# A new order for the opening of a fused gated-recurrence and ELU kernel

## The chip, the cores and the metric

The kernel runs on one NeuronCore of one Trainium2 chip. The metric is the device time of one execution in microseconds. Three timed runs of the kernel before took 670.13, 671.49 and 674.26 us; their median is 671.49.

A core has five engines that run their own instruction lists in order and meet at semaphores: TensorE (PE; its weight loads are shown as PEld), VectorE (DVE), ScalarE (ACT), GpSimd (POOL) and SyncE (SP), which issues most of the DMAs.

## The reference

The inputs q, k, v, a_re and a_im have the shape 4 x 8 x 768 x 48 (batch, head, time, feature), and the weights are 384 x 2048 and 2048 x 384. The weights arrive as 64-bit floats.

```python
mag = np.sqrt(a_re * a_re + a_im * a_im)
scale = np.minimum(mag, 0.999) / (mag + 1e-06)
a_re_n, a_im_n = a_re * scale, a_im * scale
for t in range(S):
    ar, ai = a_re_n[:, :, t, :, None], a_im_n[:, :, t, :, None]
    S_re, S_im = ar * S_re - ai * S_im + outer(k[t], v[t]), ar * S_im + ai * S_re
    y[:, :, t] = q[:, :, t] @ S_re
x = y.transpose(0, 2, 1, 3).reshape(3072, 384)
h = x @ w_in
out = np.where(h > 0, h, np.exp(np.minimum(h, 0)) - 1) @ w_out
```

The first part is a linear recurrence with a complex decay per step and feature. The second is a two-layer network with an ELU between the layers.

## The kernel before

**Units.** The work is cut into 12 units. A unit is 128 time steps of two batches, thus 256 rows of x. For a unit u the kernel turns the recurrence into products within chunks of 64 steps and a state that is carried from chunk to chunk. Its steps are small functions, each called with u and, where a unit is done by halves, the batch n:

- load_a, load_qk, load_v: DMAs from SP (L598).
- squares, joined, logarithms, powers, lengths, ratios, slopes (L705 to L780): the logarithm of the decay's size and the tangent of its angle, on ScalarE and VectorE. noted (L791) checks the range of the inputs on ScalarE.
- angles (L811 or L815): the arctan, on ScalarE. carried (L826) adds the turns that the unit before left.
- decays (L932 or L889, with the exponentials L920 or L904): sums over time as products with a triangular matrix, then the exponentials of both signs.
- turns (L837 on TensorE, L842 to L849 on VectorE): the sums of the angles; carry_on (L862) keeps the last row for a later unit with a DMA from POOL.
- waves (L973 to L977): sine and cosine on ScalarE. ends (L946 to L954): the decay over a whole chunk, as small products, two small copies and a product.
- scaled (L982 to L992) and gated (L1003): q and k times decay and wave, on VectorE.
- transposed (L1023, copies L1024), scores (L1031, mask L1036), states (L1064, sums L1077 to L1081), values (L1100 and L1109, copies L1121 and L1126): the attention-like products. scored and valued are the forms of unit 2 and later, which treat both halves together (L1136, L1145, L1177).
- seam (L1190): DMAs that put the last features of a head pair into the rows of x.

**The network.** For the first two units (u = 0, 1) the first layer is inner(u, f) on TensorE (L1210, 12 instructions of 128 x 256, two blocks of 128 hidden columns) and elu(u, f) (L1219, L1220 on ScalarE, L1221 on VectorE). project(u, n, f0, f1) adds the second layer for some blocks (L1235) and writes the output (copies L1243, DMAs L1244). Later units use sums of blocks that save products (mult L1455, product L1319, with sums of the weights in combined L1278 and summed_in L1403).

**Weights.** fetch loads a part of the 64-bit weights, and convert is one instruction of five on VectorE (L40, L43, L46, L50, L655) that round a part to 32 bits. There are 16 parts: eight of w_in, eight of w_out. inner(u, 2m) needs part m of w_in; a chunk of project needs two parts of w_out.

**Buffers.** PSUM holds three banks called w (transposes, scores, states, sums), three called mlp (inner, the projections of unit 0, sums and warm) and two called y (values, the projections of unit 1). inner(u, f) can only start when an elu has freed a bank.

**Order.** Nothing is scheduled by a planner in the opening. The list first (L1584) names the steps in the order in which they are written, and each engine's instruction list has its instructions in that order; an instruction that has to wait holds all that stand behind it on its engine. table (L1200) loads a set of ScalarE's functions ahead of use; where none is named, a load is put in before the function that needs it. warm (L1557) is some products of no use that keep TensorE's clock up. What the list doesn't name is appended from a second list with planned times (plan), in the order of those times; this is the steady part, from unit 3 on, of about 50 us per unit.

## Time and profile before

| | |
|---|---|
| median of three runs | 671.49 us |
| the profiled execution | 669.23 us |
| its span | 667.1 us |
| TensorE busy, share | 639.6 us, 96% |
| VectorE busy, share | 503.6 us, 75% |
| ScalarE busy, share | 419.2 us, 63% |
| GpSimd busy, share | 154.4 us, 23% |
| mean granted TensorE clock | 0.993 |
| first inner of unit 0 | 41.70 us |
| first inner of unit 1 | near 79 us |
| last convert on VectorE ends | near 128 us |
| first inner of unit 2 | near 164 us |

The profile is one execution, recorded in hardware. The span is from its first to its last instruction, and the profiled execution's own time is that and 2.1 us around it. A row of a timeline has its start and its duration in microseconds, engine, line, operation, what is written and read, the shape, how many instructions are merged, and in brackets the idle time of the engine before it with what ended it. Durations of one engine can overlap a little at their ends, so distances between starts are used for sums. The busy time of TensorE is modelled at the ends; a full TensorE need not be one at its peak.

### The profile page before, as it was taken

To read this page: it belongs to the slowest core of one execution; us is meant where nothing else is said; L and a number is where in the kernel's file an instruction comes from. 1 tells how busy PE (TensorE), PEld (TensorE's weight loads), DVE (VectorE), ACT (ScalarE), POOL (GpSimd) and SP (SyncE) were. 2 spreads that over 40 slices of the span, in tenths; PEclk is the share of its full clock that TensorE was granted. 3 is DMA by queue.
4 is the path that set the end of the run, shared out by engine and by line. 5 is a ranking of instruction groups with operands and counts; after the bars stand their busy time and mean duration, and the time that the engine had idled before them with its cause. 6 is when DMAs were issued, how large, how long until landed. Compare 5 with 4: busy or idle time off the path is not lost.

```text
span 667.1 us, 17231 instructions
## 1 busy us (share of the span) xinstructions
PE 639.6 (96%) x7236; PEld 579.6 (87%) x7236; DVE 503.6 (75%) x801; ACT 419.2 (63%) x684; POOL 154.4 (23%) x200
## 2 busy tenths in 40 slices
PE   8899899999999899999999999999999999999995
PEld 6777786576898798998998998999999999999995
DVE  5889999968777788678678768768768768765481
ACT  6885455874846567667677677677677577471250
POOL 2000000112124303503503503503603602402000
PEclk9799999999999999999999999999999999999999
DMA  9986645630900632452451451451551551212100
GB/s 166 189 142 105 148 149 167 112 72 20 154 3 15 115 56 62 81 106 57 86 106 53 90 104 48 97 104 44 100 104 44 102 104 43 54 32 61 34 2 29
DMA packets 151443, 56.12 MB, mean 84 GB/s; under 512 B 129684, under 2 KB 143164, under 8 KB 151356
## 3 DMA queue, kind: packets, MB, share of 16 engines
q1 hardware_dynamic: 147616, 53.58, 38.8%
q0 software_dynamic: 3520, 1.20, 1.5%
q8 instruction: 59, 0.97, 0.6%
q14 instruction: 28, 0.23, 0.1%
q10 hardware_dynamic: 220, 0.14, 0.1%
HBM read 48.91 MB, written 4.80 MB: 81 GB/s over the span
## 4 chain that ended last, share of the span: by engine, by line
PE 44%; DVE 10%; ACT 8%; issue 3%; DMA 1%; SPq 0%; ACTq 0%; DVEq 0%
PE mlp L1319 18%; PE mlp L1455 10%; PE y L1455 5%; DVE g L1471 3%; PE w L1023 3%; DVE g L1480 3%; PE y L1109 2%; ACT ee L1477 2%; ACT ee L1476 2%; PE w L1064 2%; PE w L837 2%; DVE g L1297 1%; ACT L735 1%; DVE n L772 1%; ACT n L746 1%
## 5 line engine op out<-in xcount | busy, mean ns | idle before, releaser
L1319 PE MATMUL mlp<-w_out,g 128*128 128x192 f32 x640 | 111.8, 328 | 1.0 <-DVE ee L1331 1.0
L1319 PEld LDWEIGHTS mlp<-w_out,g 128*128 128x128 f32 x640 | 104.2, 190 | 4.4 <-DVE ee L1331 1.6
L1081 POOL TENSOR_TENSOR S<-S,T 128x384 f32<-128x384 f32 x36 | 30.9, 857 | 175.5 <-DVE S L1079 175.5
L1210 PE MATMUL mlp<-x,w_in 128*128 128x256 f32 x288 | 65.1, 381 | 3.0 <-DVE g L1221 2.6
L1210 PEld LDWEIGHTS mlp<-x,w_in 128*128 128x128 f32 x288 | 53.8, 190 | 11.7 <-DVE g L1221 3.1
L1471 DVE TENSOR_TENSOR g<-g,mlp 128x512 f32<-128x512 f32 x45 | 30.7, 682 | 40.1 <-ACT qt L1024 28.7
L1297 DVE TENSOR_TENSOR g<-g 128x512 f32<-128x512 f32 x80 | 54.4, 695 | 5.0 <-PE mlp L1319 3.8
L1455 PE MATMUL mlp<-x,w_in 128*128 128x128 f32 x424 | 56.2, 275 | 0.4 <-DVE o L1344 0.4
L1480 DVE SCALAR_TENSOR_TENSOR g<-ee,g 128x512 f32<-128x512 f32 x63 | 47.6, 755 | 11.1 <-ACT ee L1477 11.0
L1319 PE MATMUL mlp<-w,g 128*128 128x192 f32 x320 | 54.5, 329 | 0.0
L1319 PEld LDWEIGHTS mlp<-w,g 128*128 128x128 f32 x320 | 51.8, 190 | 0.6
L1455 PEld LDWEIGHTS mlp<-x,w_in 128*128 128x128 f32 x424 | 51.6, 192 | 0.8 <-DVE o L1344 0.6
L1476 ACT ACTIVATE ee<-g 128x512 f32<-128x512 f32 x63 | 39.5, 627 | 17.2 <-DVE g L1471 16.7
L1190 POOL DMA_DIRECT2D x<-y x62 | 29.8, 488 | 87.2 <-ACT y L1126 37.3
L1468 ACT COPY g<-mlp 128x512 f32<-128x512 f32 x36 | 21.1, 586 | 44.0 <-PE mlp L1455 43.7
L1477 ACT ACTIVATE ee<-ee 128x512 f32<-128x512 f32 x72 | 45.4, 631 | 2.3
L1024 ACT COPY qt<-w 128x512 f32<-128x512 f32 x48 | 25.8, 589 | 15.5 <-PE w L1023 15.4
L973 ACT ACTIVATE cs<-n 128x768 f32<-128x768 f32 (+1 forms) x14 | 10.5, 751 | 38.0 <-DVE n L845 37.9
L904 ACT ACTIVATE n<-w 64x384 f32<-64x384 f32 (+1 forms) x60 | 28.1, 486 | 8.9 <-PE w L889 8.3
L1455 PE MATMUL mlp<-x,g 128*128 128x128 f32 x224 | 29.7, 275 | 1.2 <-DVE o L1344 1.2
L1219 ACT ACTIVATE ee<-mlp 128x512 f32<-128x512 f32 x24 | 14.3, 595 | 25.6 <-PE mlp L1210 17.2
L1455 PE MATMUL y<-x,w_in 128*128 128x128 f32 x216 | 29.0, 277 | 1.4 <-ACT g L1468 1.4
(222 smaller groups left out, 1434.8 us busy)
## 6 DMA issues: line engine op xcount, KB each, us to landing
w<-in_moe_w_out_dram SPq DMA_DIRECT2D x8, 768.0 KB
g<-in_moe_w_in_dram SPq DMA_DIRECT2D x24, 256.0 KB
g<-in_moe_w_out_dram SPq DMA_DIRECT2D x24, 256.0 KB
w<-in_moe_w_in_dram SPq DMA_DIRECT2D x16, 288.0 KB
vn<-in_v_dram SPq DMA_DIRECT2D x24, 192.0 KB
ar<-in_a_re_dram SPq DMA_DIRECT2D x22, 192.0 KB
ai<-in_a_im_dram SPq DMA_DIRECT2D x22, 192.0 KB
q<-in_q_dram SPq DMA_DIRECT2D x22, 192.0 KB
```

Of the source, the lines that this page charges most:

```text
L904: nc.scalar.activation(out=flat(x[key][to, n : n + 1]), in_=t[of], func=AF.Exp, scale=sign)
L1024: nc.scalar.copy(out=o[:, h0 : h0 + 4], in_=t)
L1081: eng.tensor_tensor(out=new_s, in0=new_s, in1=wide, op=ALU.mult)
L1190: eng.dma_start(out=x["x"][ds(j * HP + D, G), i], in_=x["y"][ds(j * HP + i * G, G)])
L1210: nc.tensor.matmul(t[:, e], lhsT=w_in[:, i, ts(f + e, C)], rhs=x["x"][:, i], start=(i == 0), stop=(i == NI - 1),)
L1297: nc.vector.tensor_tensor(out=S_of(u, k, h), in0=a, in1=b, op=op)
L1319: nc.tensor.matmul(to, lhsT=a[:, m], rhs=b[:, m], start=(first and h == 0 and m == 0), stop=False, skip_group_check=True,)
L1455: nc.tensor.matmul(x["c" + c][:, ts(m, C)], lhsT=a[:, m], rhs=x["mix"][p], start=(p == BANKS[c][0] and m == 0), stop=False, skip_group_che ...
L1471: nc.vector.tensor_tensor(out=part(u, to), in0=part(u, a), in1=part(u, b), op=op)
L1476: nc.scalar.activation(out=e, in_=part(u, of), func=AF.Relu, scale=-1.0)
L1477: nc.scalar.activation(out=e, in_=e, func=AF.Exp, scale=-1.0)
L1480: nc.vector.scalar_tensor_tensor(out=part(u, to), in0=nat[u]["e", to], scalar=-1.0, in1=part(u, of), op0=ALU.add, op1=ALU.max,)
```

## The change

Only the list first changes. The functions are the same, and the same steps are issued, each once, in another order:

- Unit 0: the halves of k are scaled in the other order and ahead of ends; a convert step stands ahead of gated; q of batch 0 is transposed first, then k of batch 0, q of batch 1; the natural_log set is loaded after the first two; states(0, 0) comes ahead of scores(0, 1); the logarithms of unit 1 come behind values(0, 0).
- Unit 1: slopes and angles come ahead of noted, and ends, turns and scaled ahead of inner(0, 0) and inner(0, 2). elu(0, 0) comes behind waves. The set trig_and_small is named ahead of waves for the units 1, 2 and 3. transposed(1, "q", 1) comes ahead of inner(0, 6).
- The first layer: elu(0, 4) comes ahead of seam(1); other elus and inners change places.
- The projections: unit 1's first two chunks come ahead of inner(1, 14) and unit 0's first; unit 1's last chunk of batch 1 comes ahead of unit 2's states.
- Unit 2: its four transposes stand next to each other. Unit 3: its turns and waves come later among the projections, its q and k loads behind the first outputs.
- The list goes on a little further, with steps of the units 2 to 4 that the plan put in nearly the same order before.

The core of the diff, with "..." where lines are left out:

```diff
-        (waves, 0, 1), (begun, 1), (warm, 1), (scaled, 0, "q", 0), (ends, 0), (scaled, 0, "k", 0),
-        (scaled, 0, "k", 1), (scaled, 0, "q", 1), (warm, 1), (gated, 0, 0), (warm, 1), (noted, 0),
-        (table, "natural_log"), (warm, 2), (gated, 0, 1), (warm, 2), *3 * [(convert,)],
-        (transposed, 0, "k", 0), (transposed, 0, "q", 1), (carry_on, 0), (transposed, 0, "q", 0),
-        *4 * [(convert,)], (scores, 0, 0), (transposed, 0, "k", 1), (scores, 0, 1), (load_a, 1),
-        (squares, 1), (joined, 1), (fetch, "in", 3), (logarithms, 1), (states, 0, 0),
-        (values, 0, 0), (powers, 1), (convert,), (states, 0, 1), (lengths, 1), (load_qk, 1),
-        (convert,), (ratios, 1), (values, 0, 1), (seam, 0), (warm, 2), (warm, 2), (decays, 1),
-        (load_a, 2), (warm, 1), (inner, 0, 0), *2 * [(convert,)], (noted, 1), (scaled, 1),
-        (warm, 4), (convert,), (load_v, 1), (slopes, 1), (ends, 1), *3 * [(convert,)],
-        (inner, 0, 2), (elu, 0, 0), (convert,), (fetch, "in", 4), (angles, 1), (turns, 1),
-        (waves, 1), (gated, 1, 0), (inner, 0, 4), (gated, 1, 1), (transposed, 1, "q", 0),
-        (transposed, 1, "k", 0), (convert,), (scores, 1, 0), (load_v, 2), (convert,),
...
+        (turned, 0, 1), (waves, 0, 0), (waves, 0, 1), (begun, 1), (scaled, 0, "q", 0), (warm, 1),
+        (scaled, 0, "k", 1), (scaled, 0, "k", 0), (ends, 0), (scaled, 0, "q", 1), (warm, 1),
+        (noted, 0), (convert,), (gated, 0, 0), (warm, 1), (warm, 2), (gated, 0, 1), (warm, 2),
+        (convert,), (transposed, 0, "q", 0), (convert,), (transposed, 0, "k", 0),
+        (table, "natural_log"), (carry_on, 0), (transposed, 0, "q", 1), (scores, 0, 0),
+        *3 * [(convert,)], (load_a, 1), (transposed, 0, "k", 1), (states, 0, 0), (scores, 0, 1),
+        (squares, 1), (joined, 1), (fetch, "in", 3), (convert,), (values, 0, 0), (logarithms, 1),
+        (powers, 1), (convert,), (states, 0, 1), (warm, 2), (load_qk, 1), (convert,), (lengths, 1),
+        (values, 0, 1), (ratios, 1), (seam, 0), (warm, 2), (decays, 1), (load_a, 2), (warm, 1),
+        (slopes, 1), (convert,), (angles, 1), (convert,), (noted, 1), (convert,), (ends, 1),
+        (load_v, 1), (convert,), (turns, 1), (scaled, 1), (inner, 0, 0), (convert,), (inner, 0, 2),
+        (fetch, "in", 4), (table, "trig_and_small", 1), (warm, 4), (waves, 1), (gated, 1, 0),
+        (convert,), (elu, 0, 0), (convert,), (transposed, 1, "q", 0), (gated, 1, 1),
+        (transposed, 1, "k", 0), (load_v, 2), (convert,), (inner, 0, 4), (convert,),
+        (fetch, "in", 5), (scores, 1, 0), (states, 1, 0), *2 * [(convert,)],
+        (transposed, 1, "k", 1), (convert,), (transposed, 1, "q", 1), (fetch, "in", 6),
+        (inner, 0, 6), *2 * [(convert,)], (elu, 0, 2), (convert,), (fetch, "in", 7), (scores, 1, 1),
+        (convert,), (values, 1, 0), (states, 1, 1), (values, 1, 1), *3 * [(convert,)], (warm, 2),
+        (elu, 0, 4), (seam, 1), (convert,), (inner, 0, 8), *2 * [(convert,)], (inner, 0, 10),
+        (elu, 0, 8), (convert,), (fetch, "out", 0), (elu, 0, 6), (convert,), (inner, 1, 0),
...
+        *3 * [(convert,)], (elu, 1, 12), *4 * [(convert,)], (project, 1, 0, 0, 4),
+        (project, 1, 1, 0, 4), (inner, 1, 14), (project, 0, 0, 0, 4), (logarithms, 2), (convert,),
...
+        (table, "trig_and_small", 2), *3 * [(convert,)], (project, 1, 0, 8, 12), *2 * [(convert,)],
+        (turns, 2), (project, 0, 1, 4, 8), (begun, 3), *2 * [(convert,)], (waves, 2), (squares, 3),
+        (scaled, 2), (ends, 2), (gated, 2), (joined, 3), (project, 1, 1, 8, 12),
+        (project, 1, 1, 12, 16), (logarithms, 3), (powers, 3), (states, 2, 0), (load_qk, 3),
+        (project, 1, 0, 12, 16), (lengths, 3), (ratios, 3), (project, 0, 0, 8, 12),
+        (transposed, 2, "k", 0), (transposed, 2, "q", 1), (slopes, 3), (transposed, 2, "q", 0),
+        (transposed, 2, "k", 1), (table, "trig_and_small", 3), (angles, 3), (scored, 2), (opened,),
+        (carried, 3), (project, 0, 1, 8, 12), (valued, 2), (seam, 2), (noted, 3),
+        (project, 0, 0, 12, 16), (summed_in, 0), (summed_in, 1), (combined, 1, 1), (turns, 3),
...
```

## The prediction

> **What bounds the kernel now.** I read the page's slices first, then TensorE's, VectorE's and ScalarE's instructions in order of time over the opening (0 to 165 us), the only part in which the change moves anything.
>
> The page, part 2, busy tenths of 40 slices of 16.7 us:
>
> ```profile
> PE   8899899999999899999999999999999999999995
> DVE  5889999968777788678678768768768768765481
> PEclk9799999999999999999999999999999999999999
> ```
>
> TensorE is full from the sixth slice to the end, so time is saved only where it idles, warms up or runs at half clock, which is in the first 104 us; from there on its order decides nothing unless a new hole opens. The stretches of 10 us (busy PE, PEld, DVE, ACT, POOL) show the second bound:
>
> ```profile
> 20.00:30.00 10.00, 8.67 (x73) 7.86 (x72) 9.79 (x14) 7.92 (x14) 0.00 (x0) 0.67 1.13 184
> 60.00:70.00 10.00, 9.34 (x265) 8.19 (x267) 9.58 (x15) 5.17 (x12) 0.00 (x0) 1.00 0.70 119
> 90.00:100.00 10.00, 10.00 (x48) 8.80 (x47) 9.79 (x15) 5.91 (x10) 0.00 (x0) 1.00 0.51 160
> ```
>
> From 50 to 130 us VectorE is 88 to 98% busy converting the weights (16 parts of 0.57 + 0.96 + 0.55 + 0.96 + 0.96 = 4.0 us) beside the units' gates. A change of order takes no work from it. The holes of TensorE, from its timeline:
>
> ```profile
> 41.70 3.06 PE L1210 MATMUL mlp<-x,w_in 128*128 128x256 f32 x12 [0.36 <-DMA x<-y]
> ...
> 55.44 1.09 PE L1023 MATMUL w<-ident,qg 128*128 128x128 f32 x8 [0.92 <-DVE qg L1003]
> ...
> 75.94 2.86 PE L1210 MATMUL mlp<-x,w_in 128*128 128x256 f32 x12 [2.65 <-DVE g L1221]
> 78.63 0.61 PE L1557 MATMUL mlp<-ident 128*128 128x128 f32 x4
> 79.08 23.48 PE L1210 MATMUL mlp<-x,w_in 128*128 128x256 f32 x108
> 103.98 2.85 PE L1235 MATMUL mlp<-w_out,g 128*128 128x384 f32 x8 [1.42 <-DVE g L1221]
> ```
>
> The two large holes end with VectorE's L1221 (the elu that frees an mlp bank). All gaps from 20 to 104 us add up to 8.8 us. On ScalarE:
>
> ```profile
> 46.07 1.28 ACT L815 ACT_TABLE_LOAD   x1
> 47.37 0.84 ACT L815 ACTIVATE n<-n 128x768 f32<-128x768 f32 x1
> 48.23 1.28 ACT L973 ACT_TABLE_LOAD   x1
> 52.70 0.52 ACT L973 ACTIVATE cs<-n 128x384 f32<-128x384 f32 x1 [3.19 <-DVE n L845]
> ```
>
> Unit 1's arctan (L815) stands behind noted and the first elu; its sine waits 3.19 us for the turns.
>
> **What the Trainium skill says.** "ScalarE: Activation LUTs", What ACT_TABLE_LOAD costs: a switch of set loads for about 1283 ns; the rows above show 1.28 us. "TensorE: Matmul & The Clock Gate", Part 1: the clock is halved after a window of some 3.4 us with TensorE idle and freed after a busy one; the trace agrees, with a granted clock of 0.50 from 20 to 26 us, right after the small products of ends at 16.55 to 19.3. "DMA: Bandwidth & Descriptors", Latency and other measured facts: about 2 us of fixed cost; the page's median for the seam's POOL copies (x<-y) is 2.0.
>
> **The change, part by part.** I lay the new order out with the old durations: VectorE by start-to-start distances (0.47 us for 384 columns, 0.87 to 0.99 for 768, 0.60 for an elu), TensorE 2.65 us for an inner or a project of four, 0.87 for a transposed; all from the rows of before.
>
> *Unit 0 (20 to 39 us).* q0 and k0 are transposed first, and the natural_log load goes behind their copies. The transposes run at half clock until 26.5 (1.73 us each instead of 0.87), so scores(0,0) starts at 27.1 for 27.70: 0.6 gained. Then states(0,0) goes ahead of scores(0,1), and unit 0's last product ends at 37.8 for 38.7. One convert step (0.55) ahead of gated is paid later anyway. But on ScalarE the copies of values(0,0), which wait for TensorE until 32.9, now stand ahead of unit 1's logarithms: L747 ends at 39.0 for 38.1, and the copies and seam of values(0,1) behind it come 0.8 late (issued 40.1 for 39.36). That is the new wait; behind it stand decays' exponentials, 41.6 for 40.9, after the two issues (1.50 us).
>
> *Unit 1 (39 to 60 us).* decays is even (39.7 for 39.66). slopes and angles come ahead of noted and elu(0,0): arctan ends at 45.3 for 48.2, the turns start on TensorE at 45.5 for 50.5, the waves end at 50.9 for 55.2, and gated(1,0) starts at 51.6 for 54.4. The named trig load replaces one that stood there, so no load is added (36 in the first 400 instructions of ScalarE in both). inner(0,0) and (0,2) now follow the turns, hence TensorE reaches the transposes at 52.8. inner(0,4) still goes ahead of scores(1,0): 57.4 for 57.75. Of almost 3 us only 0.35 is left at this place, and VectorE, which has done the same work, is level within 1 us. noted(1) ends at 47.4 for 44.5 and releases unit 1's a buffer, so the fetch of the fifth weight part goes out at 47.5 for 46.99: free, as its first use is at 62.
>
> *First layer (60 to 109 us).* values(1,1) ends at 70.1 for 70.5. The warm calls are as many as before, one pair only stands earlier. elu(0,4) now runs ahead of seam(1), so the bank that ended the 2.65 us hole is freed earlier: inner(0,10) at 73.7 for 75.94. The seam's three issues (2.73 us on ScalarE) follow it to 75.2, elu(0,8) is late by that, and inner(1,0) starts at 77.3 for 79.08. From here the free banks pace TensorE: VectorE ends the eighth part at 84.4 for 84.0, and inner(0,12), (0,14), (1,10) each wait 0.1 to 0.3 for an elu; inner(1,12) ends at 101.0 for 103.0. The 1.42 us hole goes, because two chunks of unit 1's projection (their weights converted by 93.3) stand where unit 0's chunk waited. After equal work (inner(1,14) and two chunks) TensorE is at 108.9 for 111.9: **3.0 us ahead.**
>
> *Unit 2 (109 to 164 us).* VectorE is as late as before: last convert 128.6 for 128.3, gated(2) for k ends 135.1 for 134.95. TensorE gets there at 135.0 with 11 chunks done for 10, so one chunk (2.65) is kept and the rest of the lead goes into the gate. Then the four transposes of unit 2 stand together, not among chunks. Three banks, emptied by copies of 0.54 us, stretch them and the state products behind them from 4.6 to 5.9 us, 1.3 lost for 0.5 before. Balance: 2.65 - 0.2 - 0.8 = **1.6 us**, inner(2,0) at 162.5 for 164.12. The seam of unit 2 is issued near 157 and lands before 161. Later gates keep up: waves(3) ends at 166.1 for 168.7.
>
> *Queues.* SP's order is the same up to unit 3's a loads. Then q and k of unit 3 go behind the outputs of the first half of unit 1: those copies end at 135.5, and the loads wait for gated(2) until 136.8 anyway (136.65 before). v of unit 3 and a of unit 4 go ahead of the last two outputs: earlier, and nothing waits for those outputs but the next o copies. POOL's carry of unit 3 goes behind the seam of unit 2 to about 161.5; its reader is at 202.6. If the cover of the q and k loads failed, their landing would still have 25 us before scaled(3).
>
> **Sum.** The profiled execution took 669.23 us (span 667.1, 2.1 around it); minus 1.6 gives 667.6. The median of the three runs is 2.3 above the profiled one and I shift by that: 671.49 - 1.6 = **669.9**. From 164 us the order is the old one and the lead passes through, as TensorE waits there under 4 us in all, for things that itself set going. Not shown by the trace is how many of the waits of 0.1 to 0.3 add up; with the lengths of copies and issues that makes 1.3 either way.
>
> **Rivals.**
> (1) *Larger gain, 667.0.* If the copies on ScalarE cost less than laid out and gated(2) ends before TensorE arrives, the lead of 3.0 at 109 us survives, and the small holes at 41.7 and 55.4 (1.3 together) go too: 4.3 to 4.5. For it: both large holes are attacked. Against: VectorE has no idle time to give, and it sets the gate at 135.
> (2) *Slower: a second half-clock stretch, 673.3.* Moving inner(0,0) behind the turns leaves TensorE from 41 to 45.5 us with one warm instruction and the small products of ends (L946), and an idle wait for the copy once; that is the pattern that came before the half clock at 20 us. A stretch like that one (6.7 us) loses up to 3.4 us of products (turns, inner(0,0), inner(0,2)): +3.4 - 1.6 = +1.8. It decides if over 3.2 us run at half clock with none of it hidden. Against: VectorE is the second bound, so half of it may be hidden, and then the result is rival 3.
> (3) *Nothing moves, 671.4.* The gate at 135 us comes 1.5 us later, as VectorE waits for late scores(1,0), and eats the chunk.
>
> **How the numbers follow.** Forecast 0.48, larger gain 0.17, slower 0.2, nothing 0.15. The forecast's own range is 668.6 to 671.2; rival 1's 667.0 and rival 2's 673.3 with the runs' own spread give 666.9 to 673.4. A measurement tells about 1% from no change (the runs before spread 0.6%), 6.7 us: no case reaches it, the largest conceivable gain (all 8.8 us of gaps) just would; I leave 0.03 for faster and 0.04 for slower from a hole that I don't see.
>
> **What would show it.** Right: turns of unit 1 near 45.5, gated(1,0) near 51.6, no hole above 1.5 us from 70 to 104, inner(1,0) near 77.3, states(2,0) near 135 with 11 chunks done, inner(2,0) near 162.5. Wrong: a granted clock of 0.5 after 43 us, ScalarE's copies holding scores, a wait for qg or kg at 135 of over 1 us, or a hole in front of the transposes of unit 3.

## The result, and the profile after

The changed kernel took 667.18 us (median; 665.14 to 668.96) where the kernel before took 670.23 us beside it (668.52 to 674.26), 20 runs each; the two medians are 3.05 us apart. The ratio of the two kernels is 0.9947, with a 95% interval of 0.9936 to 0.9959: a gain of 0.5%, or 3.5 us (2.8 to 4.3) of the median on record, where the prediction had 1.6. The direction and "within 1%" held. But 667.18 lies under the forecast's own range (668.6 to 671.2) and only within the wide one (666.9 to 673.4): the size was short by a factor of two. The profiled execution of the changed kernel took 665.7 us (span 663.7, before 669.23 and 667.1).

The same views as before the change. The page, part 2, in 40 slices of 16.6 us:

```profile
PE   8889999999999899999999999999999999999995
...
DVE  5798999967868689578678678678668768764481
...
PEclk9799999999999999999999999999999999999999
```

The stretches of 10 us (busy PE, PEld, DVE, ACT and POOL, then the granted clock):

```profile
20.00:30.00 10.00, 9.38 (x80) 8.85 (x79) 7.92 (x12) 7.62 (x14) 0.00 (x0) 0.70 1.19 176
60.00:70.00 10.00, 9.92 (x263) 8.52 (x260) 8.54 (x13) 4.25 (x10) 0.00 (x0) 1.00 0.53 100
90.00:100.00 10.00, 10.00 (x48) 8.80 (x47) 9.76 (x14) 6.17 (x10) 0.00 (x0) 1.00 0.48 156
```

In the first stretch TensorE is busier (9.38 for 8.67 us) but hardly further along (scores(0, 0) start at 27.20 for 27.70), for its clock is at half again (0.70 for 0.67). VectorE is less busy in the second (8.54 for 9.58), because it now waits for TensorE there:

```profile
60.81 0.69 DVE L1036 TENSOR_TENSOR a<-w,mask 128x512 f32<-128x512 f32 x1 [1.15 <-PE w L1031]
```

TensorE of the changed kernel in order of time (start, duration, then the idle time before the row and what ended it):

```profile
45.66 0.41 PE L953 MATMUL w<-once,pair 48*128 48x32 f32 x2 [1.94 <-DVE once L951]
46.00 2.43 PE L837 MATMUL w<-n,sum_turns 128*128 128x384 f32 x4
48.22 6.21 PE L1210 MATMUL mlp<-x,w_in 128*128 128x256 f32 x24
...
55.16 1.04 PE L1023 MATMUL w<-ident,qg 128*128 128x128 f32 x8
...
72.21 29.18 PE L1210 MATMUL mlp<-x,w_in 128*128 128x256 f32 x132
101.23 5.32 PE L1235 MATMUL y<-w_out,g 128*128 128x384 f32 x16
106.39 2.75 PE L1210 MATMUL mlp<-x,w_in 128*128 128x256 f32 x12
...
134.59 1.15 PE L1064 MATMUL w<-vn,kg 64*64 64x48 f32 x64
...
140.93 1.04 PE L1023 MATMUL w<-ident,kg 128*128 128x128 f32 x8
...
144.75 1.53 PE L1064 MATMUL w<-vn,kg 64*64 64x48 f32 x64
...
161.43 7.93 PE L1210 MATMUL mlp<-x,w_in 128*128 128x256 f32 x36
```

Four things are to be seen. The turns of unit 1 (L837) start at 46.00 instead of 50.48, but take 2.43 us for 1.45, and inner(0, 0) and inner(0, 2) behind them 6.2 us for 5.3: half clock. The transposes of unit 1 start at 55.16, before 55.44: of the 4.5 us by which the turns are earlier, 0.3 are left. From 72.21 us eleven inner steps stand in one row (132 products) without a hole; before, there was a hole of 2.65 us in this stretch and one of 1.42 us right behind it. And states(2, 0) starts at 134.59 with eleven chunks of the projections done, before at 135.01 with ten.

ScalarE, the arctan of unit 1 and its first sine:

```profile
44.49 0.84 ACT L815 ACTIVATE n<-n 128x768 f32<-128x768 f32 x1
...
48.62 0.52 ACT L973 ACTIVATE cs<-n 128x384 f32<-128x384 f32 x1
```

The arctan ends at 45.3 for 48.2 and the sine starts at 48.62 for 52.70, as laid out.

### The profile page after: what moved, and what is told of

Same layout as the page of the kernel before. It is cut to its first block, busy times and chain, and to the rows that moved or that the text cites. A ratio compares the mean times of both kernels' runs of the same rounds, so it can differ in the third digit from the quotient of the medians.

```text
span 663.7 us, 17229 instructions
## 1 busy us (share of the span) xinstructions
PE 640.6 (97%) x7236; PEld 580.2 (87%) x7236; DVE 501.9 (76%) x801; ACT 418.9 (63%) x684; POOL 153.8 (23%) x200
## 4 chain that ended last, share of the span: by engine, by line
PE 63%; DVE 14%; ACT 10%; issue 5%; DMA 4%; SPq 3%; DVEq 0%; ACTq 0%
PE mlp L1319 20%; PE mlp L1455 10%; PE mlp L1210 7%; PE y L1455 5%; PE w L1023 4%; DVE g L1471 4%; PE mlp L1235 3%; PE y L1235 3%; PE y L1109 3%; DVE g L1480 3%; SPq L598 3%; DMA w<-in_moe_w_in_dram 3%; PE w L1064 2%; PE w L837 2%; ACT ee L1477 2%
## 5 line engine op out<-in xcount | busy, mean ns | idle before, releaser
L1471 DVE TENSOR_TENSOR g<-g,mlp 128x512 f32<-128x512 f32 x45 | 30.6, 681 | 40.1 <-ACT qt L1024 28.6
L1455 PEld LDWEIGHTS mlp<-x,w_in 128*128 128x128 f32 x424 | 51.6, 192 | 0.7 <-DVE o L1344 0.6
L1190 POOL DMA_DIRECT2D x<-y x62 | 29.9, 489 | 94.8 <-ACT y L1126 43.5
L1468 ACT COPY g<-mlp 128x512 f32<-128x512 f32 x36 | 21.1, 585 | 43.9 <-PE mlp L1455 43.7
L1079 DVE TENSOR_TENSOR S<-w,S 128x384 f32<-128x384 f32 x38 | 21.0, 553 | 12.2 <-POOL S L1081 10.0
```

The source lines that it names most:

```text
L1190: eng.dma_start(out=x["x"][ds(j * HP + D, G), i], in_=x["y"][ds(j * HP + i * G, G)])
L1455: nc.tensor.matmul(x["c" + c][:, ts(m, C)], lhsT=a[:, m], rhs=x["mix"][p], start=(p == BANKS[c][0] and m == 0), stop=False, skip_group_che ...
L1471: nc.vector.tensor_tensor(out=part(u, to), in0=part(u, a), in1=part(u, b), op=op)
```

## The experiments

Two terms first. A chunk is one call of project, four blocks for one batch, 2.6 us of TensorE. The gate of unit 2 is the moment when VectorE has kg ready, without which states(2, 0) can't start.

The theories were these. *Chain*: the lead is made between 70 and 104 us and handed through the gate of unit 2 as one chunk of work; the two losses that the prediction charged there don't exist. *Sum of parts*: each part of the change brings its own share. And on the half clock, which came as the second rival had it: *it costs time* against *VectorE hides it*. A ratio below is time over the time of the kernel before, with its 95% interval. "From L720" is the time of a checkpoint counted from the first cumulated product (L720), since executions of one kernel start up to 1.3 us apart there. The diffs, with "..." where lines are left out, are against the changed kernel where the text names no other.

**One half of the change at a time.** First the changed order up to inner(1, 12), near 101 us, with the old order behind it:

```diff
         (inner, 1, 8), (inner, 1, 10), (convert,), (inner, 1, 12),
...
-        (project, 1, 0, 0, 4), (project, 1, 1, 0, 4), (inner, 1, 14), (project, 0, 0, 0, 4),
+        (project, 0, 0, 0, 4),
...
+        (inner, 1, 14),
...
+        (project, 1, 0, 0, 4), (project, 1, 1, 0, 4),
```

> The changed order up to inner(1, 12), the old order from there on. Theory (a lead of TensorE is worth only what can be done ahead of the gate of unit 2): TensorE ends inner(1, 12) about 1.3 us earlier than before, waits longer than the old 1.42 us for the elu ahead of unit 0's first chunk, and what is left of the lead is lost in front of states(2, 0) near 135 us, because only ten chunks are due there: inner(2, 0) within 0.5 us of the old 164.1, time 0 to 0.5 us under the kernel before. Rival (the parts add up, each brings its own share): inner(2, 0) near 162.3, time 1.5 to 2 us under the kernel before.

Ratio 1.0012 (0.9998 to 1.0026): not a gain at all. TensorE's row at the place (the kernel with only the opening changed), and its clock in three stretches (the granted clock stands behind the busy time of PE):

```profile
105.06 5.49 PE L1235 MATMUL mlp<-w_out,g 128*128 128x384 f32 x8 [3.38 <-DVE g L1221]
110.33 3.19 PE L1210 MATMUL mlp<-x,w_in 128*128 128x256 f32 x12
```

```profile
104.00:106.00 2.00, 0.94 (x2) 0.60 0.27 35
106.00:108.00 2.00, 2.00 (x5) 0.50 0.87 324
108.00:110.00 2.00, 2.00 (x4) 0.50 0.09 34
```

TensorE comes to unit 0's first chunk 0.9 us earlier than before and waits 3.38 us for the elu. From 104.4 us on, near the end of that wait, the clock is 0.50 for 6.8 us, and the chunk takes 5.49 us for 2.85. The lead is lost twice.

Then the reverse, the old order up to inner(1, 12) and the changed one behind it. (Unit 1's named table load, which only the changed list has, stood behind inner(1, 12) here: two loads of 1.28 us on ScalarE, for which TensorE didn't wait. The diff is against the kernel before.)

```diff
         (inner, 1, 8), (inner, 1, 10), (joined, 2), (convert,), (inner, 1, 12),
...
-        (project, 0, 0, 0, 4), (convert,), (elu, 1, 10),
+        (elu, 1, 10),
...
+        (project, 1, 0, 0, 4), (project, 1, 1, 0, 4), (inner, 1, 14), (project, 0, 0, 0, 4),
```

> The old order up to inner(1, 12), the changed order from there on. Theory: the hole of 1.42 us in front of unit 0's first chunk goes, as two chunks of unit 1 stand there instead, and the eleventh chunk ahead of states(2, 0) carries that through the gate; TensorE reaches states(2, 0) near 136.3 us, the gate is ready by then; inner(2, 0) near 162.7, time about 1.4 us under the kernel before. Rival 1 (the order of the projections is worth nothing without the opening): within 0.4 us of before. Rival 2 (the whole gain sits here): 3 us under before.

Ratio 0.9973 (0.9957 to 0.9988), 1.8 us, where the theory gave 1.4. From the timeline of TensorE:

```profile
76.14 4.26 PE L1210 MATMUL mlp<-x,w_in 128*128 128x256 f32 x12 [2.80 <-DVE g L1221]
...
104.27 5.32 PE L1235 MATMUL y<-w_out,g 128*128 128x384 f32 x16
...
137.62 1.15 PE L1064 MATMUL w<-vn,kg 64*64 64x48 f32 x64
...
164.47 7.93 PE L1210 MATMUL mlp<-x,w_in 128*128 128x256 f32 x36
```

The first row is the old hole, here 2.80 us; but inner(0, 10) takes 4.26 us, where it took 2.86 in the profile that the prediction was made from. In this execution a stretch of half clock followed the hole. The hole of 1.42 us is gone (104.27, no wait). 1.8 us from this half and nothing from the other, against 3.5 together: the parts don't add up.

**The gate of unit 2.** The eleventh chunk behind the state products instead of ahead of them:

```diff
-        (project, 1, 1, 12, 16), (logarithms, 3), (powers, 3), (states, 2, 0), (load_qk, 3),
+        (logarithms, 3), (powers, 3), (states, 2, 0), (project, 1, 1, 12, 16), (load_qk, 3),
```

> The changed kernel with the eleventh chunk, project(1, 1, 12, 16), behind states(2, 0) instead of ahead of it. Theory (the lead is carried through the gate as this one chunk): TensorE gets to states(2, 0) near 131.9 us and waits until the gate's k is ready at 134.1 to 134.3, so 2.2 us are lost; inner(2, 0) near 163.6, time 2.2 us above the changed kernel. Rival (the gate is not the bound, or VectorE catches up): no wait, within 0.5 us of the changed kernel.

Ratio 0.9975 (0.996 to 0.999), 1.9 us above the changed kernel where 2.2 were expected. TensorE's rows:

```profile
136.01 1.43 PE L1064 MATMUL w<-vn,kg 64*64 64x48 f32 x64 [1.92 <-DVE kg L1003]
137.37 6.78 PE L1235 MATMUL y<-w_out,g 128*128 128x384 f32 x16
```

TensorE waits 1.92 us for kg, and the two chunks behind take 6.78 us for 5.32, at half clock once more. So the gate is a bound, with a chunk less; with the chunk it isn't. When it opens, VectorE tells (first the kernel before, then the changed one):

```profile
123.35 0.95 DVE L826 SCALAR_TENSOR_TENSOR n<-more,n 1x768 f32<-1x768 f32 x1 [0.91 <-ACT n L815]
...
127.38 0.96 DVE L655 TENSOR_TENSOR w_out<-wp,wf 128x768 f32<-128x768 f32 x1
...
133.19 1.76 DVE L1003 TENSOR_TENSOR kg<-k,cs 128x1536 f32<-128x1536 f32 x1
```

```profile
126.64 0.96 DVE L655 TENSOR_TENSOR w_out<-wp,wf 128x768 f32<-128x768 f32 x1
...
132.32 1.76 DVE L1003 TENSOR_TENSOR kg<-k,cs 128x1536 f32<-128x1536 f32 x1 [0.88 <-ACT cs L977]
```

The last conversion (L655) ends at 128.34 and kg at 134.95 before; 127.60 and 134.08 after. VectorE is 0.7 to 0.9 us earlier at the gate, although it then waits 0.88 us for the waves. One reason is in the first row: before, VectorE waited 0.91 us for unit 2's arctan (L815) ahead of the last conversion, and in the changed kernel it doesn't. TensorE's last chunk ahead of the gate ended at 134.9 before, together with kg, and at 134.6 after, 0.5 us behind kg.

**The four transposes side by side.** A chunk between the two pairs:

```diff
-        (project, 1, 0, 12, 16), (lengths, 3), (ratios, 3), (project, 0, 0, 8, 12),
-        (transposed, 2, "k", 0), (transposed, 2, "q", 1), (slopes, 3), (transposed, 2, "q", 0),
+        (project, 1, 0, 12, 16), (lengths, 3), (ratios, 3),
+        (transposed, 2, "k", 0), (transposed, 2, "q", 1), (project, 0, 0, 8, 12), (slopes, 3),
+        (transposed, 2, "q", 0),
```

> The changed kernel with the chunk project(0, 0, 8, 12) between the first two and the last two transposes of unit 2, instead of all four side by side. The prediction's term (the four together lose 0.8 us net): inner(2, 0) 0.8 us earlier than the 161.4 of the changed kernel. Theory after the result (the stretch was an error of mine, three banks and copies of 0.54 us keep up): inner(2, 0) within 0.3 us of 161.4, and the time with it.

Neither: ratio 0.9984 (0.997 to 0.9998), 2.5 us above the changed kernel. TensorE's rows, then ScalarE's:

```profile
140.80 0.60 PE L1023 MATMUL w<-ident,qg 128*128 128x128 f32 x4
143.65 0.66 PE L1023 MATMUL w<-ident,qg 128*128 128x128 f32 x4 [2.25 <-ACT kt L1024]
```

```profile
141.85 0.83 ACT L747 ACTIVATE n<-n 128x768 f32<-128x768 f32 x1
...
143.00 1.08 ACT L1024 COPY kt<-w 128x512 f32<-128x512 f32 x2
```

With the chunk behind them the first two transposes come 2.6 us earlier with respect to states(2, 0), while ScalarE is still at unit 3's logarithms (L746, L747) and can't empty their banks: 2.25 us of waiting. The edit thus moved the transposes in time as well, so the time of the run says nothing on the adjacency. The two traces do: transposes and second state products took 5.28 us in one piece in the changed kernel (140.93 to 146.21) and 5.16 in their pieces before.

**elu(0, 4) and the seam.** In the changed kernel the old order of the two, and in the kernel before the new one:

```diff
-        (elu, 0, 4), (seam, 1), (convert,), (inner, 0, 8),
+        (seam, 1), (elu, 0, 4), (convert,), (inner, 0, 8),
```

> The changed kernel with seam(1) ahead of elu(0, 4) again. Theory (elu(0, 4) ahead of the seam is what closes the hole of 2.65 us): a hole of 2 to 2.7 us in front of inner(0, 10), in some executions with a stretch of half clock behind it (1.4 us more); inner(1, 12) ends 2 to 3 us later than in the changed kernel, and the time is 2 to 3.5 us above it, for the gate of unit 2 is no cushion any more. Rival (the hole only moves, as VectorE's conversions set the pace of the banks): inner(1, 12) within 0.7 us, time within 0.7 us of the changed kernel.

```diff
-        (convert,), (seam, 1), *4 * [(convert,)], (inner, 0, 8), (inner, 0, 10), (elu, 0, 4),
+        (convert,), (elu, 0, 4), (seam, 1), *4 * [(convert,)], (inner, 0, 8), (inner, 0, 10),
```

> The kernel before with one step moved: elu(0, 4) ahead of seam(1). Theory (the hole of 2.65 us goes, but its lead is lost in front of unit 0's first chunk, which waits for an elu that VectorE paces, and at the gate of unit 2 with ten chunks): no hole at 76 us, a hole of 2.5 to 4 us near 104 us in place of 1.42, inner(2, 0) within 0.5 us of before or up to 2.5 us later if the longer hole is followed by half clock; time from the same to 2 us above before. Rival (each hole closed is a gain by itself): time 1.5 to 2.7 us under before.

The first: 0.9956 (0.9943 to 0.997), by the medians 0.3 and 0.8 us above the two measurements of the changed kernel. That is less than expected and nearer to the rival, though its profile shows the hole (1.95 us) and half clock behind it (77.7 to 81.1 us), with inner(1, 12) at 105.0 for 101.2; that profiled execution took 669.75 us, 1.7 more than the median of these runs. The second was a loss: 1.0037 (1.0021 to 1.0053). Its TensorE:

```profile
77.26 2.86 PE L1210 MATMUL mlp<-x,w_in 128*128 128x256 f32 x12 [1.61 <-DVE w_in L655]
81.03 0.71 PE L1557 MATMUL mlp<-ident 128*128 128x128 f32 x4 [0.91 <-DVE g L1221]
...
107.70 2.85 PE L1235 MATMUL mlp<-w_out,g 128*128 128x384 f32 x8 [2.31 <-DVE g L1221]
```

and its VectorE:

```profile
74.66 0.69 DVE L1221 SCALAR_TENSOR_TENSOR g<-ee,mlp 128x512 f32<-128x512 f32 x1 [1.14 <-ACT ee L1220]
...
76.25 0.96 DVE L655 TENSOR_TENSOR w_in<-wp,wf 128x768 f32<-128x768 f32 x1
```

The hole of 2.65 us has become 1.61 us, now for L655, the last step of a weight conversion, and 0.91 for the next elu; the hole of 1.42 us is 2.31. Together 4.8 us for 4.1. From values(1, 1) to inner(2, 0) this profile takes 95.6 us, the one of the kernel before 94.3; so about half of the loss of 2.5 us lies behind the moved step, and the rest stays open. The elu pulled ahead waits 1.14 us on VectorE for ScalarE, and the conversion stands behind it. In the changed kernel two more convert steps stand ahead of that elu, and cover its wait (it runs at 74.43 there without one). By these rows it is not the one swap that closes the hole, but the swap with the conversions ordered around it.

**The opening alone undone.** The old order up to values(1, 1), where both orders have issued the same work (27 convert steps among it), and the changed order behind it. It ran twice, the second time beside the changed kernel on one chip.

```diff
-        (transposed, 0, "q", 0), (convert,), (transposed, 0, "k", 0), (table, "natural_log"),
+        (table, "natural_log"), (warm, 2), (gated, 0, 1), (warm, 2), *3 * [(convert,)],
...
-        (slopes, 1), (convert,), (angles, 1), (convert,), (noted, 1), (convert,), (ends, 1),
-        (load_v, 1), (convert,), (turns, 1), (scaled, 1), (inner, 0, 0), (convert,), (inner, 0, 2),
-        (fetch, "in", 4), (table, "trig_and_small", 1), (warm, 4), (waves, 1), (gated, 1, 0),
+        (warm, 1), (inner, 0, 0), *2 * [(convert,)], (noted, 1), (scaled, 1),
+        (warm, 4), (convert,), (load_v, 1), (slopes, 1), (ends, 1), *3 * [(convert,)],
+        (inner, 0, 2), (elu, 0, 0), (convert,), (fetch, "in", 4), (angles, 1), (turns, 1),
+        (waves, 1), (gated, 1, 0), (inner, 0, 4), (gated, 1, 1), (transposed, 1, "q", 0),
...
         (values, 1, 0), (states, 1, 1), (values, 1, 1), *3 * [(convert,)], (warm, 2),
```

> The old order up to values(1, 1), near 70 us, and the changed order from there on (elu(0, 4) ahead of seam(1), the projections, unit 2). The same work has been issued up to that point in both orders, 27 convert steps among it. Theory (formed after the runs so far: the reordered first 70 us bring nothing, for values(1, 1) ended 1.0 us later in the changed kernel than before; the gain is made behind it): values(1, 1) 63.1 us after the first cumulated product (L720) as before, no half clock after 28 us, no hole of 2.65 us, inner(2, 0) 153.7 to 154.8 us after L720 (154.9 in the changed kernel, 157.4 before), time 3 to 4.5 us under the kernel before. Rival (the earlier angles, turns and waves are the gain): inner(2, 0) 156.5 to 157.5 us after L720, time 0 to 1.5 us under before.

> The changed kernel as it is, to compare the others with on the same chip: 0.993 to 0.996 of the time before by all theories.

> The old order of the first 70 us with the changed order behind it, on the same chip as the changed kernel. Theory (the reordered first 70 us bring nothing, as their earlier waves are paid for with half clock): within 0.8 us of the changed kernel of the same comparison, either sign. Rival (the first 70 us bring about 1 us of the 3.5): 1 us or more above the changed kernel.

Ratios 0.9957 (0.9937 to 0.9977) and, on the common chip, 0.9948 (0.9926 to 0.9969) beside 0.9942 (0.992 to 0.9965) for the changed kernel; the medians there are 667.01 and 667.70. Without the change's first 70 us the gain is the same, within what the runs can tell (about 1.5 us); inner(2, 0) comes 155.5 us after L720, a little later than the theory had it. The kernel with the old start, from TensorE's timeline:

```profile
72.67 6.50 PE L1210 MATMUL mlp<-x,w_in 128*128 128x256 f32 x28
80.05 22.68 PE L1210 MATMUL mlp<-x,w_in 128*128 128x256 f32 x104 [0.88 <-DMA x<-y]
102.57 5.32 PE L1235 MATMUL y<-w_out,g 128*128 128x384 f32 x16
...
162.78 7.93 PE L1210 MATMUL mlp<-x,w_in 128*128 128x256 f32 x36
```

No hole of 2.65 and none of 1.42 us. What it has instead is a wait of 0.88 us for the seam's copy in front of inner(1, 0), 0.6 to 1.3 us in eight of the profiles with the changed order behind values(1, 1), the changed kernel's second one among them; the first one, shown above, happens to have none.

**The half clock.** Warm products where TensorE lies nearly idle around ends of unit 1 (a step of one warm is two rows of the profile). This too ran twice, as the same kernel.

```diff
-        (values, 0, 1), (ratios, 1), (seam, 0), (warm, 2), (decays, 1), (load_a, 2), (warm, 1),
+        (values, 0, 1), (ratios, 1), (seam, 0), (warm, 2), (decays, 1), (load_a, 2), (warm, 6),
...
+            if u == 1:
+                warm(10)
             once = new("once", 1, [D, NB, C // L, H])
```

> The changed kernel with 15 more small warm products where TensorE lies nearly idle from 41 to 45.6 us: 5 ahead of ends of unit 1, 10 between its two groups of products. Theory (the half clock after 44 us costs time, 3.4 us of it in some executions and 6.7 in others): the granted clock stays at 1.00 from 28 us on, the turns of unit 1 take 1.45 us for 2.43, inner(1, 12) ends near 100.4 us counted from the same start, and the median is 1 to 2 us under that of the changed kernel. Rival (VectorE sets the pace there and hides the half clock, as one of the prediction's cases has it): the clock stays up, but the time is within 0.4 us of the changed kernel.

> The changed kernel with the 15 warm products around ends of unit 1 a second time, beside the changed kernel and the kernel with the old first 70 us on one chip. Theory (the second stretch of half clock is part of the changed kernel's time and goes with the warm products): 0.8 to 2 us under the changed kernel of the same comparison. Rival (hidden behind VectorE): within 0.5 us of it.

The clock is full from 26 us on, and the turns take 1.56 us (TensorE's rows of the second run, then one of its VectorE):

```profile
44.34 2.50 PE L1559 MATMUL mlp<-ident 128*128 128x128 f32 x20
46.77 0.41 PE L955 MATMUL w<-once,pair 48*128 48x32 f32 x2
47.10 1.56 PE L837 MATMUL w<-n,sum_turns 128*128 128x384 f32 x4
```

```profile
47.21 0.19 DVE L956 COPY T<-w 128x32 f32<-128x32 f32 x1 [1.88 <-PE w L955]
```

Ratios 0.9928 (0.9901 to 0.9955) and 0.9930 (0.9907 to 0.9954), medians 666.18 and 666.65. By the ratios that is 1.3 and 0.8 us under the changed kernel, at the lower end of what was expected, and the best of all versions. That it beats the kernel before is shown; that it beats the changed kernel is likely but not shown, as the intervals overlap.

The traces say what the half clock costs here. Counted from scores(0, 0), the last products of values(1, 1) start after 43.7 us in the three profiles of this opening whose stretch near 45 us is 3.4 us long, after 44.9 to 45.1 in the three with 6.8 us, and after 43.5 in both with the warm products. So at this place the short stretch is nearly hidden and the long one costs 1.4 us: both theories hold in part. The warm products have a price too: the product of ends (L955) stands behind them, and VectorE waits 1.88 us for it, 0.50 and 0.72 in the two profiles of the changed kernel.

With useful work in the same place: inner(0, 0) between the two groups of products of ends (which takes a part for it) and five warm products more ahead of them; and then inner(0, 4) moved ahead of the transposes too:

```diff
-        (values, 0, 1), (ratios, 1), (seam, 0), (warm, 2), (decays, 1), (load_a, 2), (warm, 1),
-        (slopes, 1), (convert,), (angles, 1), (convert,), (noted, 1), (convert,), (ends, 1),
-        (load_v, 1), (convert,), (turns, 1), (scaled, 1), (inner, 0, 0), (convert,), (inner, 0, 2),
+        (values, 0, 1), (ratios, 1), (seam, 0), (warm, 2), (decays, 1), (load_a, 2), (warm, 6),
+        (slopes, 1), (convert,), (angles, 1), (convert,), (noted, 1), (convert,), (ends, 1, 0),
+        (inner, 0, 0), (ends, 1, 1), (load_v, 1), (convert,), (turns, 1), (scaled, 1),
+        (convert,), (inner, 0, 2),
```

> The changed kernel with inner(0, 0) between the two groups of products of ends of unit 1 (it waits for nothing but the seam of unit 0, which lands near 43 us), and 5 more warm products ahead of ends. Theory: TensorE is busy from 43.7 us on, no half clock, the turns start near 46.8 us and end as before near 48.3, inner(0, 2) ends at 51 for 54.3, the transposes of unit 1 start when VectorE has their gate (53.3 for 55.2), scores(1, 0) at 57.7 for 59.6; inner(1, 12) 1 to 2 us earlier than 101.2, and the time 1 to 2.5 us under the changed kernel. Rival (VectorE hides it all): within 0.4 us of the changed kernel.

```diff
-        (convert,), (elu, 0, 0), (convert,), (transposed, 1, "q", 0), (gated, 1, 1),
-        (transposed, 1, "k", 0), (load_v, 2), (convert,), (inner, 0, 4), (convert,),
+        (convert,), (elu, 0, 0), (convert,), (inner, 0, 4), (transposed, 1, "q", 0), (gated, 1, 1),
+        (transposed, 1, "k", 0), (load_v, 2), (convert,), (convert,),
```

> As the kernel with inner(0, 0) inside ends, with inner(0, 4) also ahead of the transposes of unit 1, in the place where TensorE would then wait for the gate. Theory: inner(0, 4) from 51 to 53.7 us, the transposes behind it without a wait, scores(1, 0) near 55.6, VectorE's waits of 1.15 and 0.37 us near 60 us go; inner(1, 12) near 99.5 us, time 2 to 3.5 us under the changed kernel. Rival (VectorE hides it, or the lead is lost at the gate of unit 2, for which eleven chunks are then too few): time within 0.5 us of the kernel with inner(0, 0) inside ends alone.

Both missed: 0.9957 (0.9943 to 0.9971) and 0.9952 (0.9939 to 0.9966), no better than the changed kernel. The row in which each lost it (first the one, then the other):

```profile
54.46 1.58 PE L1027 MATMUL w<-ident,qg 128*128 128x128 f32 x8 [2.17 <-DVE qg L1007]
```

```profile
61.17 1.94 PE L1027 MATMUL w<-ident,kg 128*128 128x128 f32 x8 [1.91 <-DVE a L1040]
```

The work done early leaves a hole later, for qg in the one and for VectorE's a in the other, and about its end the clock fell to half for 3.4 us (54.9 to 58.3, and 61.2 to 64.7 us). The half clock moved with the hole.

Last, four more warm products around ends of unit 0, in the kernel with the old start, against which the diff is, to do away with the first stretch of half clock:

```diff
-        (begun, 1), (warm, 1), (scaled, 0, "q", 0), (ends, 0), (scaled, 0, "k", 0),
+        (begun, 1), (warm, 3), (scaled, 0, "q", 0), (ends, 0), (scaled, 0, "k", 0),
...
+            if u == 0:
+                warm(2)
             once = new("once", 1, [D, NB, C // L, H])
```

> As the kernel with the old order up to values(1, 1) and the changed one behind it, with four more warm products around ends of unit 0 (two ahead of it, two between its groups of products), where TensorE lies nearly idle before the first stretch of half clock. Theory (the half clock follows a window with too few products): the granted clock stays above 0.9 from 19 to 28 us, the transposes of unit 0 take 1.04 us for 1.94, scores(0, 0) start 1 to 1.5 us earlier, time 0.5 to 1.5 us under the kernel without them. Rival (four products are too few, or the start is bound by VectorE and ScalarE): clock 0.5 again for 3.4 to 6.7 us, or the same time within 0.4 us.

The rival was right: 0.9948 (0.9931 to 0.9966), the same as without. The first stretch lasted 3.4 us, scores(0, 0) came 20.2 us after L720 for 21.2, but stretches of 6.8 us at 36 and of 3.4 us at 50 us followed. The clock fell at 18.9 us although TensorE counts as busy for 2.86 of the 3 us ahead of it; over half of that time went to products of two columns (L946, 1.64 us).

**The kernel before, profiled three more times.**

> The kernel before, unchanged, profiled once more. Theory (the profile that the prediction was made from was one of its better executions: the hole of about 2.7 us ahead of inner(0, 10) is followed by half clock in others): a granted clock of 0.5 for some 3.4 us behind that hole, or a second stretch between 40 and 55 us, in at least two of three looks; inner(2, 0) 158.5 to 161 us after the first cumulated product (L720), for 157.4. Rival (that profile was typical): no half clock after 28 us, 157 to 158 us.

> As the first look: by the theory half clock behind the hole or between 40 and 55 us in at least two of three, by the rival in none.

> As the first look: by the theory half clock behind the hole or between 40 and 55 us in at least two of three, by the rival in none.

The clock in the third of these profiles, c below, where a wait of 2.25 us for VectorE's S ends at 35.4 us (busy PE, then the granted clock):

```profile
35.00:37.00 2.00, 1.64 (x30) 0.83 1.33 145
37.00:40.00 3.00, 3.00 (x50) 0.50 0.83 136
40.00:43.00 3.00, 3.00 (x38) 0.50 0.03 8
```

The profiles of the kernels that are compared here, as read from TensorE's timeline and clock. The first column of times has the start of the last products of values(1, 1); the last column lists the stretches at half clock, without the one at the very end:

| kernel | values(1, 1), from L720 | inner(2, 0), from L720 | half clock, us |
|---|---|---|---|
| before, on record | 63.1 | 157.4 | 6.8 at 19.7 |
| before, a | 63.7 | 158.0 | 6.8 at 21.5 |
| before, b | 69.9 | 165.0 | 10.2 at 18.3, 10.2 at 35.4, 3.4 at 52.5, 3.4 at 83.2 |
| before, c | 66.0 | 160.4 | 3.4 at 19.3, 6.8 at 36.3 |
| changed | 64.3 | 154.9 | 6.8 at 19.2, 3.4 at 46.5 |
| changed, again | 64.5 | 156.8 | 3.4 at 20.8, 6.8 at 44.7 |
| old start, new rest | 64.1 | 155.5 | 6.8 at 20.7 |
| old start, new rest, again | 63.8 | 155.2 | 6.8 at 19.9 |
| changed, warm products | 63.0 | 154.7 | 3.4 at 21.2 |
| changed, warm products, again | 64.3 | 155.6 | 3.4 at 21.7 |

The profile that the prediction was worked out from was the best of four. Of the theory, a second stretch of half clock came in b and c, but behind the hole ahead of inner(0, 10) only in b, and inner(2, 0) fell into the stated 158.5 to 161 only in c. The difference of the two columns shows where the gain is made: from values(1, 1) to inner(2, 0) it is 94.3 to 95.1 us in the four profiles of the kernel before and 90.6 to 92.3 in the six with the changed order there, whichever start they have and however long they ran at half clock ahead of it.

## Why the prediction was right or wrong

The path was forecast rightly: no hole ahead of the projections, and eleven chunks done when unit 2's state products start. What failed is the size, at two terms of the sum (−0.2 and −0.8) and at the base (+2.3). A third step failed in unit 1, and in the other direction: it made the gain smaller.

**Unit 0: right.** scores(0, 0) at 27.20 (27.1 forecast), seam(0) issued at 40.00 (40.1), the exponentials at 41.54 (41.6).

**Unit 1: right up to the turns, wrong behind them.** Arctan 45.3 (45.3), turns 46.0 (45.5), waves to 50.9 (50.9), gated(1, 0) 52.31 (51.6). But the transposes came at 55.16 (52.8), scores(1, 0) at 59.61 (57.4) and values(1, 1) ended at 71.5 (70.1). The step that failed is that TensorE's products from 45.5 to 52.8 us were laid out at full clock, though the prediction's own second rival described the half clock at this place. Of the 2.4 us at the transposes, 0.5 is the later start of the turns and 1.9 is half clock (the turns 2.43 us for 1.45, the inner steps 6.2 for 5.3). Half clock of 3.4 or 6.8 us was there in all six profiles with this opening. In the time of the kernel it is worth what the warm products won back, about 1 us and not clear of the noise, and not the 3.4 of the rival; the result didn't end on the rival's side.

**First layer: right, the exact end by luck.** inner(1, 0) at 77.9 (77.3), inner(1, 12) to 101.23 (101.0), the lead after equal work 2.9 us (3.0), both holes gone. But TensorE came out of values(1, 1) 1.4 us later than laid out, and then the wait of about 1 us that the prediction had ahead of inner(1, 0) didn't come in this execution: two errors that cancel. The prediction gave the start 0.4 us of the lead (values(1, 1) 70.1 for 70.5). It brings nothing that can be seen: the kernels with the old start reach the first chunk 95.0 and 95.3 us after L720, the changed one 94.7 and 96.6, the kernel before 97.2 to 104.8 in four profiles.

**"VectorE is as late as before", "the rest of the lead goes into the gate" (−0.2): wrong.** The last conversion was forecast for 128.6 and ended at 127.60, kg for 135.1 and was ready at 134.08. VectorE's waits from 40 us up to the last conversion add up to 2.6 us before (0.74, 0.50, 0.47 and the 0.91 for the arctan) and to 2.0 after (0.50, 1.15 and 0.37); with 0.22 us from an earlier start of that execution, that is about the 0.74 by which the conversion is earlier. With the eleventh chunk TensorE still comes 0.5 us behind the gate, so the whole lead passes: 3.07 us at states(2, 0), the 0.22 of the start among them.

**"1.3 lost for 0.5 before" (−0.8): wrong in size.** The transposes and state products took 5.28 us, not 5.9, against 5.16 before. From states(2, 0) to inner(2, 0) 0.38 us of the lead were lost in all. So the sum "2.65 − 0.2 − 0.8 = 1.6" is 2.65 + 0.2 − 0.38 = 2.47 us, which is what the two profiles show from L720 to inner(2, 0) (157.38 for 154.91). The rest of the 3.4 us between their spans is the 0.22 of the start and 0.71 behind inner(2, 0), less than the 0.9 by which that last part differs among all profiles.

**"I shift by that" (+2.3): too much by 1.3.** Over 20 runs the kernel before has a median of 670.23 us, so its profiled execution lies 1.0 under it and not 2.3; the median of three runs was 1.3 too high by chance. Of the 2.7 us between the forecast of 669.9 and the measured 667.18 this is the one half, and the gain (3.05 for 1.6, by the medians) the other. The clock tells why the profiled execution was a good one: in 51 runs of the kernel before, measured on one chip beside the changed orders, the granted clock goes from 0.982 (674 us) to 0.994 (668 to 670 us), and the profiled one had 0.993. It doesn't tell the two kernels apart. The mean clock is 0.990 in these 51 runs and 0.990 in the 20 of the changed kernel, which is only steadier (0.989 to 0.991). So the two lose about as much to half clock, and the gain is not half clock saved. What the medians are apart beyond the 2.47 us of the two openings, 0.6, is within what executions differ by.

**From 164 us "the lead passes through": right.** From inner(2, 0) to the end it took 502.3 to 503.2 us in all profiles, whatever stood ahead of it.

**Rivals.** The larger gain (667.0) is what came, and for one of the reasons it gave: gated(2) ended before TensorE arrived, and the lead of 3.0 us survived the gate. Of its other ground, the holes at 41.7 and 55.4, the second is gone, but TensorE now waits 1.94 us near the place of the first. "Nothing moves" fell with the gate at 134.1, though VectorE did wait for scores(1, 0) as it said (1.15 us).

## What to carry to other kernels

A lead of one engine is worth what it can be handed on as: here moving the elu of the first hole alone lost 2.5 us, the new order of the projections alone won 1.8, the new opening without it won nothing, and with everything behind 70 us changed together it was 3 to 3.5. A closed hole paid only where work stood ready at the next gate. Where a profile shows half clock once, profile several executions before taking one as the baseline, and take the median of the baseline from more than three runs.

## What the runs showed of the hardware

The half clock comes in pieces of 3.4 us (3.4, 6.8 or 10.2 in all 19 profiles, the stretch at the very end left out), and the same program gets it at different places in different executions. The stretches at full clock between them are whole multiples of 3.41 us too (13.65 or 20.48 us, for example). So within one execution all changes of the clock lie on one grid of 3.41 us, and the grid lies differently in each: in the four profiles of the kernel before the clock first falls 13.0, 14.1, 12.2 and 12.7 us after L720. "TensorE: Matmul & The Clock Gate", Part 1 of the Trainium skill, says that the window which decides is free-running and doesn't start with the kernel; that agrees with these four, which have 6.8, 6.8, 27.2 and 10.2 us at half clock.

The page speaks of an idle window of some 3.4 us. Here far less did it: of thirteen waits of 1.9 us or more in full-clock stretches behind 30 us (those inside ends of unit 1 left out), eight had half clock set in about their end (1.91, 1.92, 1.95, 2.17, 2.25, 2.55, 2.80 and 3.38 us long), and five did not (2.25, 2.31, 2.62, 2.65, 2.71). Length doesn't part them, but the grid does. Each of the eight left TensorE idle for 1.9 to 2.7 us within one step of the grid, and at the end of that step the clock fell. Each of the five was cut by a line of the grid and left at most 1.6 us idle in either step. With small products in the step less was enough: around ends of unit 1, 1.2 to 1.5 us of idle time were followed by half clock in three profiles. At 20 us in the kernel before, where the prediction saw the page's rule confirmed, TensorE had been busy for 2.3 of the 3.4 us ahead.

A wait of 2 us in front of TensorE thus has two prices, its own length or that and 1.4 us more, which is what inner(0, 10) paid in 4.26 us for 2.86; where it falls on the grid decides which. And time in which TensorE counts as busy didn't protect it in the kernel with four more warm products (2.86 of 3 us), where over half of that time went to products with two columns each.
